# Order of the last block's routing and the second expert tile's split, and which engine splits two tiles' second weights

## The chip, the cores and the metric

The kernel runs on one core of one Trainium2 chip. The metric is the device time of one execution in microseconds (us); the time of the kernel before is the median of three runs. All inputs and the output lie in the chip's memory.

## The reference, cut to what matters

Three stages follow each other over 3072 tokens of width 256.

```
# 1. a state-space attention, chunk by chunk -> x, 3072 x 256
# 2. a dense layer
h = x @ w_in                      # 256 -> 2048
x = max(0.01 * h, h) @ w_out      # 2048 -> 256
# 3. a layer of 8 experts, one expert per token
logits = x @ w_gate + modality_bias[modality_id]
e_idx  = argmax(logits)
gate_w = softmax(logits)[e_idx]   # with 1e-9 in the sum
for e in range(8):                # w1: 8 x 256 x 1024, w2: 8 x 1024 x 256
    rows = (e_idx == e)
    out[rows] = gate_w[rows] * (max(x[rows] @ w1[e], 0) @ w2[e])
```

Everything is float32. Every product is made on TensorE from two halves: a high part `hi` (rounded to the type that TensorE reads) and a low part `lo = raw - hi`; three matmuls (hi x hi, hi x lo, lo x hi) make one product.

## The kernel before, in words

**Stages and blocks.** The tokens are cut into six blocks of 512. Per block and per 128 columns of the hidden layer, `mm1` (line 585) makes six matmuls into `h`, ScalarE and VectorE turn `h` into `gh` and `gl`, and `mm2` (line 605) makes six matmuls into `y`. The attention of the next block is threaded through this loop. A dictionary `sched` (line 926) says after which `mm1` each other step is written; lines 984 to 994 are the loop.

**Routing of a block.** `evict_y` copies the block's `y` out of PSUM to `yt`. `logits` (line 626) makes 16 small matmuls `lp`, copies them (`lt`), transposes them (`l`) and calls `route` (line 641): ten small VectorE instructions `lg` to the reciprocal into `ysb`, with one ScalarE exponential `ex` among them; `oh` and `ohb` hold the chosen expert. `ranks` (line 668) counts with small matmuls `rp` which place each token has in its expert's list, and four GpSimd scatters write the token's number into the list `il`. `rows` (line 702), called twice per block, transposes `yt` back to one row per token (`yr`) and ScalarE copies it to `ysb`; `rows_out` (line 713) writes `ysb` to the table of rows `yx`. `table_early` (after block 4) and `table_final` (line 766, after block 5) work out, from the counts, which expert and which list position each expert tile has.

**Expert tiles.** The expert layer is worked in tiles of 256 rows of one expert. Twelve are always done: five from the early table (tokens of the first five blocks), seven from the final one; more are done under a condition at the end. A tile has these steps: `m2_idx` (line 794) loads the tile's list entries (`gi`) and gathers its rows from `yx` (`xg`); `m2_w` (line 782) loads the weights to `r1` and `r2` through SyncE's queue; `m2_xT` (line 827) transposes the rows (`xps`) and splits them into `x2h` and `x2l`; `m2_split1` (line 812) splits the first weights into `w1s`; `m2_split2` (line 821) splits the second weights into `w2s`, in two halves; `m2_mm1` (line 840) makes 48 matmuls into `hp`, with ScalarE and VectorE making `hh` and `hl` from it; `m2_mm2` (line 859) makes 48 matmuls into `o`, and the result is scaled and scattered to the output. A split (line 525) is one ScalarE copy for the high part and one subtraction for the low part. The subtraction runs on VectorE for `w1s` and for the first half of `w2s`, on GpSimd for the second half of `w2s`, in every tile.

**Where the change sits.** After the loop over blocks the list `fin` (lines 998 to 1001) orders the steps of the last block (`jl`, block 5) and of the first two tiles. With the three positions inserted it reads: evict_y, logits, m2_xT of tile 1, ranks, table_final, rows 0, rows 1, m2_mm1 of tile 0, rows_out, m2_split1 of tile 1. The loop of lines 1005 to 1017 then writes, per tile: `m2_mm1(i)`, `m2_xT(i+1)`, `m2_split1(i+1)`, the loads for tile i+2, `m2_mm2(i)`, `m2_split2(i+1)`. Tile 0's `m2_split2` is written inside the loop over block 5 (line 980), tile 1's in the first pass of the loop over tiles.

**What sets the order.** The program is handed to a planner that orders each engine's instructions by its own estimate of when their inputs are there; the written order decides between instructions that are ready. An instruction called through `v`, `s`, `g` or `t_` (VectorE, ScalarE, GpSimd, TensorE) is tied behind the one written before it on the same engine when the step's name stands in `pin` with that letter (lines 64 to 95, `run` in line 172). In `fin` this ties VectorE's instruction of `m2_xT`, TensorE and ScalarE in `rows`, VectorE, ScalarE and GpSimd in `table_final` and `evict_y`, and ScalarE in `m2_split1`; `logits`, `ranks` and `m2_mm1` are tied by nothing. Once planned, each engine runs its queue in order. `lp`, `xps` and `yr` share one PSUM buffer (tag "m", one buffer): a later one of them waits until the one before has been read.

Of the kernel before, what the change touches and what calls it, by code (L numbers as in the profile page):

```python
# [24 lines left out]
Q = {'sg': (0, 1),  # L25
 'i00': 0,
 'i01': 1,
 'lo1': -1,
 'o00': 0,
 'o01': 4,  # L30
 'i10': 3,
 'i11': 3,
 'xe': 2,
 'se': 8,
 'me': 7,
 'sh1': -2,
 'sh': 0,
 'ld': 9,
# [60 lines left out]
def kernel(  # L99
# [70 lines left out]
    v, s, g, t_ = Pinned(nc.vector, "v"), Pinned(nc.scalar, "s"), Pinned(nc.gpsimd, "g"), Pinned(nc.tensor, "t")  # L170
# [354 lines left out]
    def split(raw, hi, lo, eng):  # L525
        s.copy(out=hi, in_=raw)
        eng.tensor_tensor(out=lo, in0=raw, in1=hi.bitcast(F32), op=ALU.subtract)
# [77 lines left out]
    def mm2(j, f):  # L605
        n = blocks[j][1]
        if f == 0:
            y_t[j] = [psy.tile([P, 512], F32, tag="y", name="y") for _ in range(2)]
        gh, gl = g_t.pop((j, f))
        for k in range(2):  # L610
            ds = slice(k * P, (k + 1) * P)
            for i, (w, gg) in enumerate(((woh, gh), (woh, gl), (wol, gh))):
                t_.matmul(y_t[j][k], lhsT=w[:, f, ds], rhs=gg, start=(f == 0 and i == 0), stop=(f == NF - 1 and i == 2))
# [207 lines left out]
    def m2_split2(i):  # L821
        d = m2[i]
        for k in range(2):
            ks = slice(4 * k, 4 * k + 4)
            split(d["r2"][:, ks, :], d["w2"][:, ks, 0, :], d["w2"][:, ks, 1, :], v if k == 0 else g)

    def m2_xT(i):
        d = m2[i]
# [148 lines left out]
    for i in range(EARLY):  # L977
        at(L + 1, m2_idx, i, tabe, i)
    at(L + 4, m2_split1, 0)
    at(L + 6, m2_split2, 0)  # L980
    at(L + 9, m2_w, 1, tabe, 1)
    at(L + Q["xt"], m2_xT, 0)
# [12 lines left out]
    jl = nb - 1  # L995
    mm2(jl, NF - 2)
    mm2(jl, NF - 1)
    fin = [(evict_y, jl), (logits, jl), (ranks, jl), (table_final,), (rows, jl, 0), (rows, jl, 1), (rows_out, jl)]
    fin.insert(Q["xe"], (m2_xT, 1))
    fin.insert(Q["se"], (m2_split1, 1))  # L1000
    fin.insert(Q["me"], (m2_mm1, 0))
    for fn, *args in fin:
        run(fn, args, "L_")
    tl = [(tabe, k) for k in range(EARLY)] + [(tabf, k) for k in range(NSTAT)]
    for i in range(len(tl)):
        if i:
            run(m2_mm1, (i,), "L_")
            if i + 1 < len(tl):
                run(m2_xT, (i + 1,), "L_")
                run(m2_split1, (i + 1,), "L_")  # L1010
        if i + 2 < len(tl):
            if i + 2 >= EARLY:
                m2_idx(i + 2, *tl[i + 2])
            m2_w(i + 2, *tl[i + 2])
        run(m2_mm2, (i,), "L_" if i + 1 < len(tl) else "Z_")
        if i + 1 < len(tl):
            run(m2_split2, (i + 1,), "L_")
    u = nc.values_load(tabu, min_val=0, max_val=NFIN, skip_runtime_bounds_check_because=WHY)

    def cond(k):  # L1020
        if k >= NFIN:
            return
        with tc.If(u > k):
            i = EARLY + k
            m2_idx(i, tabf, k)
            m2_w(i, tabf, k)
            m2_split1(i)
            m2_split2(i)
            m2_xT(i)
            m2_mm1(i)  # L1030
            m2_mm2(i)
            cond(k + 1)
# [34 lines left out]
```

## Time and profile before

| | us |
|---|---|
| median of three runs | 552.48 (550.47 to 555.38) |
| the profiled execution, its own time | 552.29 |
| its span, first to last instruction | 550.6 |
| TensorE busy in the span | 519.3 (94%) |
| VectorE busy | 365.0 (66%) |
| ScalarE busy | 334.0 (61%) |
| GpSimd busy | 199.2 (36%) |

1.7 us of the profiled execution's time lie around its span. TensorE is PE, VectorE is DVE, ScalarE is ACT, GpSimd is POOL, SyncE is SP; PEld is TensorE's weight load, which overlaps its matmuls. The expert tiles fill the last 150 us of the span; a tile's 48 matmuls `hp` are followed by its 48 matmuls `o`.

### The profile page before, as it was taken

How to read it: one execution, taken by the hardware profiler on the slowest of the kernel's cores; microseconds unless marked ns; L12 is line 12 of the kernel's file. 1: busy time of each engine (PE TensorE's matmuls, PEld its weight loads, DVE VectorE, ACT ScalarE, POOL GpSimd, SP SyncE). 2: the span in 40 equal slices, each digit the busy share in tenths (PEclk: the TensorE clock that was granted, in tenths of full speed). 3: DMA queues.
4: the chain of work that ended last, by engine and by line, in shares of the span. 5: the costliest groups of instructions: out<-in, count | busy, mean ns of one | idle time of the engine just before them, and what ended most of it. 6: DMA issues, size and time to landing. Idle time of an engine off the chain costs nothing.

```text
span 550.6 us, 9529 instructions
## 1 busy us (share of the span) xinstructions
PE 519.3 (94%) x3411; PEld 422.3 (77%) x3411; DVE 365.0 (66%) x714; ACT 334.0 (61%) x699; POOL 199.2 (36%) x167
## 2 busy tenths in 40 slices
PE   6998978999999999999999999999989999999990
PEld 3434654678787878778877787688879999999990
DVE  5658998977667777775667866475577564555630
ACT  5447667675676676765766665354537665666630
POOL 5648798300301120113010301540063466556331
PEclk9559999999999999999999999999999999999996
DMA  8898753212744239322620476345059667777300
GB/s 195 138 226 160 206 143 57 54 34 34 17 116 81 59 43 107 63 59 11 130 60 0 13 139 198 98 31 86 1 187 168 222 210 239 219 236 240 109 23 21
DMA packets 128312, 61.02 MB, mean 111 GB/s; under 512 B 84545, under 2 KB 120514, under 8 KB 128258
## 3 DMA queue, kind: packets, MB, share of 16 engines
q1 hardware_dynamic: 125186, 53.94, 48.2%
q0 software_dynamic: 3072, 6.41, 3.6%
q8 instruction: 29, 0.48, 0.4%
q14 instruction: 25, 0.20, 0.2%
HBM read 53.73 MB, written 6.60 MB: 110 GB/s over the span
## 4 chain that ended last, share of the span: by engine, by line
PE 78%; DVE 8%; issue 5%; ACT 3%; DMA 2%; SPq 1%; POOL 1%; POOLq 0%; DVEq 0%; ACTq 0%
PE y L163 21%; PE h L163 21%; PE hp L163 11%; PE o L163 10%; PE psy L163 5%; PE cb L163 3%; DVE hb L163 1%; DVE gg L163 1%; DMA ct<-in_C_dram 1%; DMA raw<-in_moe_w_in_dram 1%; DVE gl L163 1%; DVE lb L163 1%; PE yr L163 1%; PE pc L163 1%; PE pb L163 1%
## 5 line engine op out<-in xcount | busy, mean ns | idle before, releaser
L163 ACT CAST gh<-gg 128x512 fp32r<-128x512 f32 x96 | 59.6, 621 | 75.6 <-DVE gg L163 74.3
L163 DVE TENSOR_TENSOR gl<-gg,gh 128x512 fp32r<-128x512 f32 x96 | 74.0, 771 | 40.6 <-ACT gh L163 40.0
L163 PE MATMUL h<-xh,wih 128*128 128x512 f32 x192 | 77.7, 408 | 3.9 <-DVE gg L163 3.9
L163 PE MATMUL y<-gl,woh 128*128 128x512 f32 x192 | 76.6, 400 | 3.6 <-DVE gl L163 3.6
L163 DVE TENSOR_TENSOR gg<-sa,h 128x512 f32<-128x512 f32 x96 | 65.3, 681 | 20.5 <-ACT sa L163 20.2
L163 POOL TENSOR_SCALAR_AFFINE_SELECT e<-e 128x1024 f32<-128x1024 f32 (+1 forms) x28 | 28.2, 1012 | 137.9 <-DMA e<-cumd 87.1
L163 PE MATMUL h<-xl,wih 128*128 128x512 f32 x192 | 75.2, 392 | 0.0
L163 PE MATMUL y<-gh,wol 128*128 128x512 f32 x192 | 75.0, 392 | 0.0
L163 PE MATMUL h<-xh,wil 128*128 128x512 f32 x192 | 75.0, 392 | 0.0
L163 PE MATMUL hp<-x2h,w1s 128*128 128x256 f32 x384 | 71.9, 283 | 0.0
L163 PE MATMUL o<-w2s,hh 128*128 128x256 f32 x384 | 69.3, 285 | 0.0
L163 ACT ACTIVATE sa<-h 128x512 f32<-128x512 f32 x96 | 57.2, 596 | 19.0 <-PE h L163 18.4
L163 DVE SCALAR_TENSOR_TENSOR hl<-hp,hh 128x512 fp32r<-128x512 f32 x48 | 33.0, 691 | 52.6 <-ACT hh L163 44.0
L163 PE MATMUL y<-gh,woh 128*128 128x512 f32 x192 | 63.3, 398 | 0.0
L163 PEld LDWEIGHTS hp<-x2h,w1s 128*128 128x128 f32 x384 | 61.1, 192 | 0.6
L163 POOL TENSOR_TENSOR w2s<-r,w2s 128x1024 fp32r<-128x1024 f32 x12 | 34.0, 2838 | 72.7 <-ACT w2s L163 48.7
L163 PEld LDWEIGHTS o<-w2s,hh 128*128 128x128 f32 x384 | 58.4, 191 | 0.4 <-issue 0.4
L163 PE MATMUL hp<-x2l,w1s 128*128 128x256 f32 x192 | 53.3, 283 | 0.0
L163 ACT ACTIVATE hh<-hp 128x512 fp32r<-128x512 f32 x48 | 28.4, 597 | 40.0 <-PE hp L163 35.0
L163 ACT ACTIVATE e<-e,ncum 128x128 f32<-128x128 f32 x160 | 51.5, 395 | 0.0
L163 PE MATMUL o<-w2s,hl 128*128 128x256 f32 x192 | 51.1, 283 | 0.0
L163 POOL DMA_INDIRECT il<-ids,pi x24 | 25.7, 1070 | 66.5 <-DVE pi L163 38.3
(205 smaller groups left out, 1012.3 us busy)
## 6 DMA issues: line engine op xcount, KB each, us to landing
r<-in_moe_w_dram SPq DMA_DIRECT2D x48, 512.0 KB
e<-cumd SPq DMA_DIRECT2D x20, 512.0 KB
raw<-in_moe_w_in_dram SPq DMA_DIRECT2D x4, 1024.0 KB
raw<-in_moe_w_out_dram SPq DMA_DIRECT2D x4, 1024.0 KB
yx<-ysb SPq DMA_DIRECT2D x6, 528.0 KB
xt<-in_x_dram SPq DMA_DIRECT2D x24, 128.0 KB
ct<-in_C_dram SPq DMA_DIRECT2D x24, 64.0 KB
bt<-in_B_dram SPq DMA_DIRECT2D x24, 64.0 KB
```

Source lines behind the costliest of these rows:

```text
L163: r = f(*args, **kw)
```

## The change

`m2_xT` of tile 1 is written before the last block's `logits`; `ranks` and `table_final` are written at the end of `fin`, behind both `rows`, `m2_mm1` of tile 0, `rows_out` and `m2_split1` of tile 1. The three positions go out of `Q`. For tiles 0 and 1 the second half of `w2s` is subtracted on VectorE instead of GpSimd; the other tiles keep GpSimd.

```
-            split(d["r2"][:, ks, :], d["w2"][:, ks, 0, :], d["w2"][:, ks, 1, :], v if k == 0 else g)
+            split(d["r2"][:, ks, :], d["w2"][:, ks, 0, :], d["w2"][:, ks, 1, :], v if k == 0 or i < 2 else g)
...
-    fin = [(evict_y, jl), (logits, jl), (ranks, jl), (table_final,), (rows, jl, 0), (rows, jl, 1), (rows_out, jl)]
-    fin.insert(Q["xe"], (m2_xT, 1))
-    fin.insert(Q["se"], (m2_split1, 1))
-    fin.insert(Q["me"], (m2_mm1, 0))
+    fin = [
+        (evict_y, jl), (m2_xT, 1), (logits, jl), (rows, jl, 0), (rows, jl, 1), (m2_mm1, 0), (rows_out, jl), (m2_split1, 1),
+        (ranks, jl), (table_final,),
+    ]
```

## Rows read from the trace of the kernel before

**Rows 1.** Stretches: length, busy time (instructions) PE, PEld, DVE, ACT, POOL; clock, DMA share, GB/s.

```profile
365.00:380.00 15.00, 15.00 (x74) 12.44 (x73) 10.29 (x12) 8.05 (x13) 3.45 (x2) 1.00 0.92 108
394.00:412.00 18.00, 15.38 (x141) 14.41 (x140) 14.35 (x42) 8.93 (x14) 9.46 (x7) 1.00 0.42 133
436.00:520.00 84.00, 84.00 (x706) 84.00 (x705) 48.42 (x57) 53.56 (x79) 47.16 (x34) 1.00 0.67 212
```

**Rows 2.** Who waited for whom on PE from 300 us on: total, times, longest.

```profile
PE rp L163 <- DVE ohb L163: 2.1, 1, 2.1
PE h L163 <- DVE gg L163: 1.2, 1, 1.2
PE yr L163 <- DVE x2l L163: 0.5, 1, 0.5
```

**Rows 3.** Timeline of PE, 394 to 418: start, length, instruction, count, idle before and releaser.

```profile
394.19 0.41 PE L163 MATMUL lp<-yt,wg 128*32 128x128 f32 x2
...
401.70 0.63 PE L163 MATMUL hp<-x2h,w1s 128*128 128x256 f32 x4
404.44 0.19 PE L163 MATMUL rp<-ohb,tris 128*128 128x32 bf16 x1 [2.11 <-DVE ohb L163]
...
405.31 0.66 PE L163 MATMUL yr<-ident,yt 128*128 128x128 f32 x4 [0.52 <-DVE x2l L163]
...
411.51 0.40 PE L163 MATMUL o<-w2s,hh 128*128 128x256 f32 x2
...
417.69 0.28 PE L163 MATMUL hp<-x2h,w1s 128*128 128x256 f32 x1
```

**Rows 4.** Timeline of DVE around the stall.

```profile
393.47 0.69 DVE L163 COPY yt<-y 128x512 f32<-128x512 f32 x1 [0.41 <-PE y L163]
...
397.09 2.35 DVE L163 TENSOR_TENSOR w1s<-r,w1s 128x1024 fp32r<-128x1024 f32 x2
399.36 3.41 DVE L163 TENSOR_TENSOR w2s<-r,w2s 128x1024 fp32r<-128x1024 f32 x1
402.69 0.18 DVE L163 TENSOR_TENSOR lg<-l,btab 128x32 f32<-128x32 f32 x1
...
404.20 0.18 DVE L163 CAST ohb<-oh 128x32 bf16<-128x32 f32 x1
...
404.60 0.66 DVE L163 TENSOR_TENSOR x2l<-xps,x2h 128x512 fp32r<-128x512 f32 x1
```

**Rows 5.** VectorE's instructions that write w2s: min/median/max ns, first and last start.

```profile
L163 DVE TENSOR_TENSOR w2s<-r,w2s x12: 1205/1220/3409, 366.8 to 523.6; 128x1024 fp32r<-128x1024 f32 x12
```

**Rows 6.** Timelines of POOL and DVE: the second halves of tiles 1 and 0.

```profile
398.88 2.81 POOL L163 TENSOR_TENSOR w2s<-r,w2s 128x1024 fp32r<-128x1024 f32 x1 [28.60 <-ACT w2s L163]
...
367.79 2.48 POOL L163 TENSOR_TENSOR w2s<-r,w2s 128x1024 fp32r<-128x1024 f32 x1 [1.82 <-ACT w2s L163]
...
368.25 2.57 DVE L163 TENSOR_TENSOR gl<-gg,gh 128x512 fp32r<-128x512 f32 x1 [0.24 <-ACT gh L163]
```

**Rows 7.** Chain that ended last, tile 2's first pass: start, us, what.

```profile
417.86 5.76 PE hp L163 x48
```

**Rows 8.** Timeline of DVE, the table's first and last instruction and tile 2's first split.

```profile
405.34 0.19 DVE L163 TENSOR_SCALAR cm<-thr 1x96 f32<-1x96 f32 x1
...
414.24 0.67 DVE L163 SCALAR_TENSOR_TENSOR hl<-hp,hh 128x512 fp32r<-128x512 f32 x1
414.84 0.15 DVE L163 CAST tabf<-vb 1x14 int32<-1x14 f32 x1
414.91 0.67 DVE L163 TENSOR_TENSOR x2l<-xps,x2h 128x512 fp32r<-128x512 f32 x1
415.51 2.34 DVE L163 TENSOR_TENSOR w1s<-r,w1s 128x1024 fp32r<-128x1024 f32 x2
```

**Rows 9.** Timelines of SP and POOL: tile 5's list entries, the last list scatter.

```profile
429.93 0.37 SPq L797 DMA_DIRECT2D gi<-il  x1
...
410.33 0.97 POOL L163 DMA_INDIRECT il<-ids,pi  x1 [0.30 <-issue]
```

More of the change, by code (lines that the diff above doesn't have):

```diff
@@ L32 @@
  'i11': 3,
- 'xe': 2,
- 'se': 8,
- 'me': 7,
  'sh1': -2,
```

## The prediction

> **What bounds the kernel now.** I read the stretches first: how much of each TensorE was busy, and at which granted clock. In the expert tiles, from 436 to 520, TensorE is busy for 84.00 of 84.00 us at clock 1.00; in block 5's loop, 365 to 380, for 15.00 of 15.00 [rows 1]. Where it is never idle, only fewer or faster matmuls would shorten the run, and the change touches no matmul's size or number. The one stretch with room is 394 to 412, the handover from block 5 to the tiles: 15.38 busy of 18.00, so 2.62 us idle. TensorE's waits say what that was: 2.1 us of `rp` for `ohb`, 0.5 us of `yr` for `x2l`, and, from 300 on, otherwise only 1.2 us in front of an `h` that the change does not touch [rows 2]. So 2.1 + 0.5 = 2.6 us is the most that removing these waits can give.
>
> TensorE's timeline shows how it came about. At 401.70 tile 1 begins with four `hp`, which need only `x2h`; the next thing in the queue is block 5's `rp`, which waits 2.11 us to 404.44; then `yr`, which waits another 0.52 us because `x2l` still reads the shared buffer; only then does `hp` go on [rows 3]. From 401.70 to tile 1's first `o` at 411.51 it takes 9.81 us, where tile 2's 48 `hp` take 5.76 [rows 3, 7].
>
> VectorE's timeline shows what they waited for. It subtracts `w1s` from 397.09 and `w2s` from 399.36, and this one half of `w2s` takes 3.41 us; then comes the chain `lg` (402.69) to `ohb` (404.20), and last `x2l` at 404.60 [rows 4]. The other halves take 1.22 us at the median [rows 5]. So tile 1, whose weights had been split, stood behind block 5's routing twice: `rp` ahead of its `hp` in TensorE's queue, and its `x2l` tied behind the routing in VectorE's.
>
> **The change, part by part.**
>
> *The rows of tile 1 ahead of the logits.* `x2l` is tied behind VectorE's instruction written before it. That was the last of the routing, which is why it starts right after it at 404.60; it becomes the copy `yt`, which ends at 393.47 + 0.69 = 394.16 [rows 4]. With 0.66 us of its own it is done at about 394.8, 7 us ahead of the 401.70 at which `hp` asks for it. The 0.5 us wait of `yr` goes, and `hp` of tile 1 can run without the routing. The price is the shared buffer: the transposes of tile 1 now hold it before `lp`, which ran at 394.19 [rows 3]. `lp` may so come 394.8 - 394.19 = 0.6 us later. Its cost to TensorE lies between 0 (the planner puts `o` of tile 0, ready then, in front) and 0.6; a gain is excluded, since nothing asked for `lp` earlier. I take 0.2, nearer to the row that has `o` ready to fill in. If this cover is gone it is the whole 0.6.
>
> *The second half of `w2s` of tiles 1 and 0 on VectorE.* Tile 1's GpSimd half ran from 398.88 to 401.69; VectorE's half, which started inside it at 399.36, ended at 402.77, 1.08 us after GpSimd's end, about the 1.22 us of an undisturbed one [rows 4 to 6]. In tile 0 the same: GpSimd from 367.79 to 370.27, and the `gl` that started at 368.25 took 2.57 us to 370.82, where an instruction of its shape takes 0.67 [rows 6, 8]. So VectorE lost 3.41 - 1.22 = 2.19 us and 2.57 - 0.67 = 1.90 us. Moving the half costs it 1.22 each time: net 0.97 and 0.68 us less. In tile 0 it is worth nothing, since TensorE is busy throughout that stretch [rows 1]; if the extra half fell badly, it would cost at most its 1.22 us. In tile 1 it lets the chain `lg` to `ohb` end about 1.0 us earlier, even if all four halves stand before it.
>
> The Trainium skill, "SBUF — State Buffer", section "SBUF: two separate sides", says that VectorE instructions with two SBUF inputs and GpSimd instructions that read SBUF lock each other out for a whole instruction. By that rule the stretches above end with the move. Were the 3.41 us the instruction's own, VectorE would instead spend 1.22 us more, and the gain below would shrink from 2.6 to about 1.4 us.
>
> *Ranks and final table last.* This moves on VectorE five small instructions of `ranks` and the table's 22, which ran between 405.34 and 414.84 among the `hl` of tile 1 [rows 8]; on TensorE eight small `rp`; on GpSimd four list scatters, of which the last ran at 410.33; on SyncE nothing, though `rows_out` no longer stands behind them. `rp` need no longer stand ahead of tile 1's `hp`, whose inputs are all there, and so the 2.1 us wait goes. Whether the planner puts it a little too early is open: between 0 and the 2.1 us of before; I take 0.1, because the instruction that ran late is the one just shortened. Nothing asks early for what is moved: the list entries of tile 5, the first that need the full list and the final table, are loaded at 429.93 [rows 9], 15 us behind the table's end and 18.6 us behind the last scatter's. That slack hides a delay of the POOL queue and of the table; past it SyncE would hold tile 5's weights up too.
>
> *The two `rows` earlier* brings two sets of four transposes and two ScalarE copies forward, the same work, and the row table to memory sooner. Nothing.
>
> **The sum.** The profiled execution took 552.29 us, 0.2 under the median of 552.48; its span is 550.6. Out of it come 2.6 us of waits; back come 0.2 (`lp`) and 0.1 (`rp`): 2.3 us. Every later tile runs without a gap, so this reaches the end whole: 552.29 - 2.3 = 550.0 us, a gain of 0.4%.
>
> **The rivals.**
>
> *VectorE becomes the bound (the gain is halved).* It is busy 14.35 of 18.00 us in this stretch [rows 1]. Tile 2's `x2l` is tied behind the last `hl` of tile 1, and `w1s` of tile 2 follows, to 417.85, just as TensorE begins tile 2 at 417.69 [rows 3, 8]: no slack. If VectorE's order stays as it was and only the 1.0 us worked out above is saved, tile 2 begins 1.0 us earlier, not 2.6: 551.3 us. For it: the tightness. Against it: the table is no longer wanted first, and `hl` come earlier. The Trainium skill, "Perfetto Trace Analysis", section "Optimizing Scalar/DVE Operations", says that a saturated VectorE may be relieved by giving work to ScalarE or even GpSimd; the moved halves go the other way, and no run here shows it.
>
> *The wait only changes its name (no change).* The written order is only a preference: the planner may again put `rp`, or the second `yr` that waits for ScalarE's copy behind the routing, ahead of `hp`. The change then does not do what it says, and TensorE idles about as long: 552.3 us. Against it: `x2l` is tied elsewhere, which no estimate can undo.
>
> *Slower: the table ahead of tile 2's weights.* `rp` goes behind all of tile 1's `hp`, which would end at about 411.5 - 2.6 = 408.9; `rp` and `ranks` end at about 410.2 (0.4 + 5 x 0.18). The table's 22 instructions, written ahead of tile 2's steps, then take some 5 us (22 of 0.15 are 3.3; the 9.65 us from first to last less four `hl` are 7.0), two late `hl` 1.3, `x2l` 0.6 and `w1s` 2.34: 419.4, where it ended at 417.85. It decides from the point at which tile 2's `w1s` ends behind 417.85; here it is 1.6 us: 553.9 us. Against it: `ohb` is ready long before, and `rp` is short.
>
> *More than the waits.* A newly planned order also closes the 1.2 us in front of `h`, or loosens block 5's loop: 548.8 us or less. The stretch that would have to give it is full.
>
> **Chances.** Forecast 0.56, halved 0.20, no change 0.11, slower 0.08, more 0.05. The forecast's own range is 549.4 to 550.5 (all of the 2.6 plus rounding, and `lp` and `rp` at 0.6 and 1.0). The runs of before spread from 550.47 to 555.38, so a median moves by a microsecond or so by itself. From 547.6 the range takes in half of "more", and to 553.2 the halved and the unchanged case with that movement; outside are the slower case and the far ends. About 1%, 5.5 us, is what a measurement of this kernel can tell from no change. No case worked out reaches it on either side: 0.05 for faster, left for a re-planned block 5, and 0.05 for slower, for a mishap in the planned order; within it 0.90.
>
> **What would show it.** Right: in the changed profile 394 to 410 shows TensorE idle for under 0.5 us; no `rp` or `yr` among its waits over 0.3 us; `x2l` of tile 1 near 394; no half of `w2s` of tiles 0 and 1 over 1.3 us and no `gl` of 2.5 us; tile 2's `hp` starting near 415. Wrong: a wait of `hp` for `w1s` of tile 2 (VectorE the bound), a wait of `yr` for `ysb` or of `lp` for `x2l` over 0.6 us (the shared buffer), a wait of `rp` for `ohb` as before, or idle time inside block 5's loop, where none was.

## The result and the profile after

The changed kernel takes 559.5 us (558.78 to 561.05, four runs) beside 553.51 for the kernel before in the same comparison: 1.011 times, interval 1.0079 to 1.0141. It is slower, where 550.0 was forecast, in a range of 547.6 to 553.2. The profiled execution took 559.1 us, its span is 557.4. A time given below is the median of all runs of a kernel, while a ratio, with its interval in brackets, is taken against runs of the kernel before made beside it and leaves out the few runs in a slower state (one in experiment 7, two in experiment 8, one of the kernel before).

Who waited for whom on TensorE from 300 us on, in the changed kernel; the three waits of before [rows 2] are all gone, and two others stand in their place:

```profile
PE o L160 <- ACT hh L160: 6.1, 1, 6.1
PE o L160 <- DVE hl L160: 1.3, 1, 1.3
```

The timeline of TensorE in the changed kernel, tile 2 (compare [rows 3]; columns as there):

```profile
416.14 0.36 PE L160 MATMUL hp<-x2h,w1s 128*128 128x256 f32 x1
...
423.93 0.39 PE L160 MATMUL o<-w2s,hl 128*128 128x256 f32 x1 [1.32 <-DVE hl L160]
...
430.81 0.80 PE L160 MATMUL o<-w2s,hh 128*128 128x256 f32 x2 [6.14 <-ACT hh L160]
431.40 0.41 PE L160 MATMUL o<-w2s,hl 128*128 128x256 f32 x1
431.62 0.63 PE L160 MATMUL o<-w2s,hh 128*128 128x256 f32 x2
```

Tile 2 begins well, and then its second pass stands still for 6.14 us. Behind the gap two `o` take 0.42 us from start to start of the next (431.62, then 432.04), where 0.24 is usual. The stretches show why (columns as [rows 1]; the clock is the third number from the end):

```profile
394.00:412.00 18.00, 17.91 (x160) 17.02 (x160) 14.57 (x40) 10.14 (x17) 3.62 (x4) 1.00 0.47 161
...
420.00:422.00 2.00, 2.00 (x19) 2.00 (x19) 1.93 (x7) 0.50 (x2) 1.55 (x3) 1.00 0.88 74
422.00:424.00 2.00, 0.68 (x7) 0.48 (x5) 1.87 (x4) 0.00 (x0) 2.00 (x1) 1.00 1.25 87
424.00:426.00 2.00, 0.67 (x4) 0.47 (x4) 0.00 (x0) 0.00 (x0) 0.13 (x1) 0.77 0.46 68
426.00:428.00 2.00, 0.00 (x0) 0.00 (x0) 0.00 (x0) 0.00 (x0) 0.00 (x0) 0.50 0.74 194
428.00:430.00 2.00, 0.00 (x0) 0.00 (x0) 0.00 (x0) 0.79 (x1) 0.00 (x0) 0.50 1.01 380
...
434.00:436.00 2.00, 2.00 (x14) 2.00 (x13) 0.11 (x1) 0.00 (x0) 0.17 (x1) 0.67 0.80 229
436.00:438.00 2.00, 2.00 (x19) 2.00 (x18) 0.00 (x0) 0.20 (x1) 0.44 (x1) 1.00 0.97 374
```

The handover, 394 to 412, is full now: 17.91 of 18.00, against 15.38 before [rows 1]. But TensorE stands still for 1.32 us from 422.6 and for 6.14 us from 424.7; its granted clock falls from 1.00 (2.4 GHz) to 0.50 (1.2 GHz), and it stays there to about 435, after work has begun again. From 430.81 to 435.03 the trace holds 19 matmuls, 0.22 us each instead of 0.12: 1.9 us lost. Between 426 and 428 no compute engine is busy at all. Only the DMA engines are, and between 420 and 426 they move 68 to 87 GB/s, after it 194 and 380.

ScalarE's timeline in the changed kernel says what everything waits for:

```profile
416.80 0.84 ACT L160 ACTIVATE o<-o,xg 128x256 f32<-128x256 f32 x2
417.52 0.59 ACT L160 CAST x2h<-xps 128x512 fp32r<-128x512 f32 x1
417.99 2.02 ACT L160 CAST w1s<-r 128x1024 fp32r<-128x1024 f32 x2
419.89 0.61 ACT L160 ACTIVATE hh<-hp 128x512 fp32r<-128x512 f32 x1
429.21 1.05 ACT L160 CAST w2s<-r 128x1024 fp32r<-128x1024 f32 x1 [8.71 <-DMA r<-in_moe_w_dram]
430.16 0.59 ACT L160 ACTIVATE hh<-hp 128x512 fp32r<-128x512 f32 x1
430.65 1.04 ACT L160 CAST w2s<-r 128x1024 fp32r<-128x1024 f32 x1
431.59 1.09 ACT L160 ACTIVATE hh<-hp 128x512 fp32r<-128x512 f32 x2
```

The `hh` are tile 2's; the `x2h` at 417.52 and the `w1s` and `w2s` behind it are tile 3's. The planner put tile 3's first copy of `w2s` in front of three of tile 2's four `hh`. That copy waited 8.71 us for its weights to land, and TensorE waited for the `hh` behind it. In the kernel before, the same stretch reads:

```profile
420.77 0.60 ACT L163 ACTIVATE hh<-hp 128x512 fp32r<-128x512 f32 x1 [1.69 <-PE hp L163]
...
423.66 0.60 ACT L163 ACTIVATE hh<-hp 128x512 fp32r<-128x512 f32 x1 [0.60 <-PE hp L163]
424.28 0.59 ACT L163 CAST x2h<-xps 128x512 fp32r<-128x512 f32 x1
424.76 2.00 ACT L163 CAST w1s<-r 128x1024 fp32r<-128x1024 f32 x2
426.66 2.00 ACT L163 CAST w2s<-r 128x1024 fp32r<-128x1024 f32 x2
```

Four `hh` first, then tile 3's copies, and the weights are there when they are wanted.

The 1.32 us in front of the first `hl` come from the same fault in VectorE's queue. In the changed kernel it subtracts tile 3's `w1s` ahead of tile 2's `hl`:

```profile
420.86 1.20 DVE L160 TENSOR_TENSOR w1s<-r,w1s 128x1024 fp32r<-128x1024 f32 x1
422.07 1.21 DVE L160 TENSOR_TENSOR w1s<-r,w1s 128x1024 fp32r<-128x1024 f32 x1
423.20 0.67 DVE L160 SCALAR_TENSOR_TENSOR hl<-hp,hh 128x512 fp32r<-128x512 f32 x1
```

**Where the 6.8 us of span went.** The two profiled executions differ already at the end of the first block (VectorE's first `yt` at 118.6 against 116.0), long before any changed instruction; at the last `yt` it is 395.78 against 393.47, 2.3 us. About 1.0 of these is work that only stands earlier: four transposes of tile 1 and five `hp` of tile 0 now run ahead of that `yt` (from it to the last `o` the trace has 1186 matmuls before and 1177 after); against it the 1.2 us wait of `h` is gone [rows 2]. From that `yt` to tile 2's first `hp` it is 20.36 us after the change and 24.22 before: 3.9 us gained, of which 2.5 are idle time that is gone, 0.6 those five `hp`, and 0.7 that the other matmuls follow each other faster (0.3 of it the 16 `lp`, which stand in one piece now). From there to the last `o` (544.67; 536.64 before) 128.5 against 119.0: 9.6 us lost, which are 1.3 + 6.1 of waits, 1.9 of half speed and 0.3 unexplained. The end behind the last `o` is 1.2 us shorter. So 2.3 - 3.9 + 9.6 - 1.2 = 6.8. Because the starts differ from run to run, the profiles below are compared from the last `yt` to the last `o`: 143.2 us before, 148.9 after.

The load that came late was asked for earlier than in the kernel before, 416.73 against 417.88. SyncE's and GpSimd's timelines in the changed kernel:

```profile
416.73 0.95 SPq L786 DMA_DIRECT2D r<-in_moe_w_dram  x2
420.33 4.38 SPq L783 DMA_DIRECT2D r<-in_moe_w_dram  x2
...
414.38 1.77 POOL L160 DMA_INDIRECT il<-ids,pi  x1 [0.30 <-issue]
```

The last list scatter ran at 414.38 to 416.15, 4 us later than before [rows 9], just ahead of that load. Two theories follow, of which each may hold alone or with the other. **Q, the queue:** the loss is the order of ScalarE's queue, where copies for tile 3 stand ahead of tile 2's `hh`. **S, the scatters:** the load is late because bulk transfers crawl after list scatters. Their rival **D** is the one of the prediction: VectorE, with two more halves and a later table.

### The profile page after: what moved, and what is told of

Read it like the earlier page. It is cut to its first block, busy times and chain, and to the rows that moved or that the text cites. A ratio compares the mean times of both kernels' runs of the same rounds, so it can differ in the third digit from the quotient of the medians.

```text
span 557.4 us, 9520 instructions
## 1 busy us (share of the span) xinstructions
PE 519.9 (93%) x3411; PEld 424.4 (76%) x3411; DVE 363.6 (65%) x716; ACT 333.5 (60%) x699; POOL 195.6 (35%) x165
## 4 chain that ended last, share of the span: by engine, by line
PE 78%; DVE 7%; DMA 5%; issue 4%; ACT 2%; POOL 1%; SPq 0%; POOLq 0%; DVEq 0%; ACTq 0%
PE y L160 21%; PE h L160 21%; PE o L160 11%; PE hp L160 10%; PE psy L160 5%; PE cb L160 3%; DMA r<-in_moe_w_dram 2%; DVE gl L160 2%; DMA e<-cumd 1%; DMA raw<-in_moe_w_in_dram 1%; DVE gg L160 1%; PE pc L160 1%; PE yr L160 1%; DVE hb L160 1%; DVE lb L160 1%
## 5 line engine op out<-in xcount | busy, mean ns | idle before, releaser
L160 DVE TENSOR_TENSOR gl<-gg,gh 128x512 fp32r<-128x512 f32 x96 | 70.9, 739 | 40.4 <-ACT gh L160 39.1
L160 PE MATMUL o<-w2s,hh 128*128 128x256 f32 x384 | 71.2, 290 | 6.2 <-ACT hh L160 6.1
L160 PEld LDWEIGHTS o<-w2s,hh 128*128 128x128 f32 x384 | 60.0, 196 | 6.8 <-ACT hh L160 6.3
L160 PEld LDWEIGHTS h<-xh,wih 128*128 128x128 f32 x192 | 36.5, 191 | 14.2 <-DVE gg L160 5.8
```

The lines of the kernel that those rows point to most:

```text
L160: r = f(*args, **kw)
```

## The experiments

**1. ScalarE's copy of the rows tied as well.** All the change, with one letter more: it ties `x2h` behind the four `hh` written before it.

```
-         'L_m2_xT': 'v',
+         'L_m2_xT': 'vs',
```

> The changed kernel with ScalarE's copy x2h of m2_xT tied, too, behind the instruction written before it: ScalarE's queue then holds all four hh of tile 2 ahead of x2h, w1s and w2s of tile 3; all else of the change stays (table last, four halves on VectorE). Theory Q (the loss is a queue: the copy of tile 3's second weights, whose load is late, stands ahead of three hh that TensorE wants): the waits of o for hh and hl (6.1 and 1.3 us) and the half-speed matmuls behind them (20 at 0.215 instead of 0.12 us, 2 us) go, so about 559.5 - 9.4 = 550 us, a ratio to before of 0.993 to 0.997. Rival D (VectorE's added halves and the table on it late, the loss forecast as a rival): a wait of hp or o for VectorE's w1s, w2s or hl of over 3 us stays and the time is 556 us or more.

550.32 us, 0.9957 of before (0.9924 to 0.9989). The long wait is gone, though not every one: `o` still waits 1.6 us for `hh`. ScalarE's timeline in this kernel:

```profile
420.90 0.60 ACT L160 ACTIVATE hh<-hp 128x512 fp32r<-128x512 f32 x1 [0.24 <-PE hp L160]
421.40 0.58 ACT L160 CAST x2h<-xps 128x512 fp32r<-128x512 f32 x1
421.86 2.01 ACT L160 CAST w1s<-r 128x1024 fp32r<-128x1024 f32 x2
428.88 1.05 ACT L160 CAST w2s<-r 128x1024 fp32r<-128x1024 f32 x1 [5.01 <-DMA r<-in_moe_w_dram]
```

The load, asked for at 415.82, is as late as in the changed kernel (13.1 us to the copy). Now it stands behind tile 2's `hh` and delays tile 3's only. VectorE's subtractions need ScalarE's copies, and so its queue changed with the tie; tile 2's four `hl` now come first:

```profile
420.06 2.47 DVE L160 SCALAR_TENSOR_TENSOR hl<-hp,hh 128x512 fp32r<-128x512 f32 x4
...
423.05 2.34 DVE L160 TENSOR_TENSOR w1s<-r,w1s 128x1024 fp32r<-128x1024 f32 x2
```

So Q holds for the two queues together, and this run does not tell them apart. D's 556 us and its wait of over 3 us did not come; experiments 3, 4 and 9 decide about its added halves and its late table.

**2. No list scatters for the last block.**

```
-        for q in range(nq):
+        for q in range(nq if j < len(blocks) - 1 else 0):
             w = g.indirect_dma_start(out=il[:], ...
```

> The changed kernel without the last block's four list scatters, so that block's tokens are missing from the lists and their output rows are not written; ScalarE's queue keeps the order of the changed kernel. Theory S (the load of tile 3's second weights is late because bulk transfers crawl, at 60 to 140 GB/s for some 8 us, after list scatters): with no scatters that load, asked for at about 416.7, runs at over 300 GB/s and lands by about 421 to 422; o waits for hh at most 1 us instead of 6.1, and the time is about 551 us. Rival (the load is late for another reason: its own small packets, or too many loads at once): it still lands near 429 and the time stays within 1 us of the changed kernel's.

The last block's tokens are then missing from the lists; the order of copies, subtractions, `hh` and `hl` on ScalarE and VectorE is that of the changed kernel.

554.48 us. The load asked for at 415.48 has landed by 419.75, 4.3 us later, with 323 GB/s in 418 to 420 where the changed kernel has 143, and 74 in the 2 us after that. No `o` waits for `hh`. So S holds for the load. The time fell by 5.0 us where S expected some 8, since VectorE's queue has the same fault. The copy on ScalarE, and the subtraction on VectorE that costs TensorE most:

```profile
419.75 1.05 ACT L160 CAST w2s<-r 128x1024 fp32r<-128x1024 f32 x1 [0.50 <-DMA r<-in_moe_w_dram]
...
422.57 3.83 DVE L160 TENSOR_TENSOR w2s<-r,w2s 128x1024 fp32r<-128x1024 f32 x1
```

The subtraction is tile 3's first half, ahead of three `hl` of tile 2, and beside GpSimd's half (422.90, 2.40 us) it takes 3.83 us instead of 1.22. `o` waits 3.9 us for `hl` in this run: 1.3 behind `w1s`, as in the changed kernel, and 2.6 behind this half. After it the clock reads 0.71 over 426 to 428 and 0.50 over 428 to 430, so a stretch at half clock comes without the late load too.

**3. The written order alone**, second halves on GpSimd as before (`v if k == 0 else g`).

> Only the new written order; the second halves of w2s stay on GpSimd in all tiles. ScalarE's planned queue has all four hh of tile 2 ahead of tile 3's copies here. Theory Q: no wait of o for hh, so the gain of the order alone is seen: rp no longer ahead of hp, but VectorE's half of tile 1 still stretched to some 3.4 us beside GpSimd's; about 550 to 552 us. Rival D with the table as the cause: the loss stays, 556 us or more, since the table is as late here.

549.44 us, 0.9935 (0.9899 to 0.9971): faster than before. The handover is full (18.00 of 18.00), and no wait of TensorE is over 0.4 us. The table is late here too, so the late table is not the loss. One step of the expectation missed: VectorE's half of tile 1 took 1.22 us (396.57), and GpSimd's, which started behind it (396.98), took 3.04. Which of the two is stretched was not worked out: in experiment 2 VectorE's started 0.33 us ahead and was the one stretched.

**4. The halves alone**, in the written order of before.

> Only the two second halves on VectorE; the written order is that of the kernel before. Theory Q: ScalarE's queue is unharmed, so no loss; VectorE's half of tile 1 takes 1.22 instead of 3.41 us, the chain to ohb ends about 1 us earlier and the 2.1 us wait of rp shrinks to 0.5 to 1.5 us: about 552 to 553 us. Rival D with the halves as the cause: a new wait on VectorE of 3 us or more, 556 us or more.

551.64 us, 0.999 (0.9955 to 1.0025): no difference that the runs show. The halves are not the loss either. The wait of `rp` for `ohb`, expected at 0.5 to 1.5 us, is gone from this profile; 0.7 us of `hp` for `x2h` and 0.4 of `yr` for `x2l` are there.

**5. Two of the four scatters.** As in 2, with 2 in place of 0.

> The changed kernel with two of the last block's four list scatters left out (half of that block's tokens are missing from the lists). Theory S with a price per scattered entry: bulk transfers crawl for about 4 us instead of 8 behind the scatters, the load of tile 3's second weights lands some 8 us after its issue (12.5 with four scatters, 4.3 with none), o waits for hh 1 to 3 us and the time lies between 554.5 (none) and 559.5 (four), at 556 to 558 us. Rival (the crawl comes with any scatter, whatever their number): landing 12 us after the issue, 559 us.

554.54 us. From issue to the copy it is 8.8 us (414.29 to 423.12), so 4.3, 8.8 and 12.5 us for none, two and four scatters of 128 entries: about 2.1 us each. `o` waits 2.5 us for `hh` and 1.3 for `hl`, together 3.8, as much as with no scatters; the order of the queues alone costs that, and so the time is not clearly higher than in 2 (1.0061, 1.0031 to 1.0092, beside 1.0035, 1.0003 to 1.0067), where 556 to 558 was expected.

**6. One move alone:** tile 1's rows ahead of the logits, all else as before.

```
-    fin.insert(Q["xe"], (m2_xT, 1))
+    fin.insert(1, (m2_xT, 1))
```

> The kernel before with one step moved: m2_xT of tile 1 ahead of logits; ranks and table where they were, second halves on GpSimd. ScalarE's planned queue has tile 3's x2h, w1s and w2s ahead of three hh of tile 2, as in the changed kernel. Theory Q: this one move is enough for the loss; o waits for hh 2 to 6 us (the scatters come earlier than in the changed kernel, so the load may land sooner), 554 to 559 us. Rival (the loss needs the late table and ranks or the halves on VectorE): 550 to 552 us, as with the order alone.

561.04 us, 1.0183 (1.012 to 1.0245), at least as slow as the whole change (1.0079 to 1.0141). ScalarE's timeline in this kernel has the fault again, with the copy of `w2s` ahead of the `hh`:

```profile
419.09 0.60 ACT L163 ACTIVATE hh<-hp 128x512 fp32r<-128x512 f32 x1
428.81 1.04 ACT L163 CAST w2s<-r 128x1024 fp32r<-128x1024 f32 x1 [9.12 <-DMA r<-in_moe_w_dram]
429.76 0.59 ACT L163 ACTIVATE hh<-hp 128x512 fp32r<-128x512 f32 x1
```

`o` waits 7.2 us for `hh`. Neither the late table nor the halves are needed for the loss. Here the scatters ended at 410.8, and the row table, asked for at 409.18, crawled in front of the weights (13 to 38 GB/s from 412 to 418). This run has a second loss, which the changed kernel has not (a row of its waits, and one of its stretches):

```profile
PE xps L163 <- issue: 2.0, 1, 2.0
...
416.00:418.00 2.00, 2.00 (x12) 2.00 (x11) 1.37 (x2) 2.00 (x4) 1.23 (x1) 0.50 1.03 38
```

Tile 3's transposes start at 413.68, 1.95 us behind the matmul before them and just when tile 2's `x2l`, which reads the shared buffer, ends (413.62); behind this wait TensorE works at half clock (416 to 418). So the 153.6 us of this profile are not the price of the ScalarE order alone.

**7. List entries of 64 bytes** in the changed kernel: 16 equal numbers instead of one.

```
-    il = dram.tile([NE * NT, 1], I32, name="il")
+    il = dram.tile([NE * NT, 16], I32, name="il")
...
-                in_=ids[:, c0 + q:c0 + q + 1], in_offset=None,
+                in_=ids[:, c0 + q, :], in_offset=None,
```

The first fill of the list grows with it, from 96 to 1536 KB, and a tile's load of its entries takes the first number of each.

> The changed kernel with list entries of 64 bytes instead of 4: a scatter writes 128 whole entries of 16 numbers, the loads of a tile's entries take the first number of each, and the fill of the list is 16 times as large (1.5 MB, early in the run). ScalarE's queue is that of the changed kernel. Theory P (the crawl is the price of 4-byte writes): it goes, the load of tile 3's second weights lands 4 to 5 us after its issue, and the time is near the one without scatters, 554 to 556 us (plus up to 2 us if the larger fill delays the start). Rival (the price goes by the number of scattered entries): still 12 us to landing, 559 us or more.

552.74 us, 1.0015 (0.9976 to 1.0054). With all four scatters in place the load lands 4.1 us after its issue (415.11 to 419.20), as with none:

```profile
419.20 1.05 ACT L160 CAST w2s<-r 128x1024 fp32r<-128x1024 f32 x1 [0.33 <-DMA r<-in_moe_w_dram]
```

So the crawl is the price of the 4-byte writes. What is left is 3.9 us of `o` waiting for `hl`, as in 2: 1.3 behind `w1s` and 2.5 behind the same half in VectorE's queue (422.19, 3.83 us).

**8. The order alone, with 64-byte entries.**

> Only the new written order (second halves on GpSimd in all tiles, as in the run of the order alone) and list entries of 64 bytes. Theories Q and P together: no wait of o for hh, and ScalarE no longer stands 3.5 us in front of tile 3's second weights; TensorE's idle of 0.7 us in 424 to 436 goes: 548.5 to 549.5 us, a ratio to before of about 0.992. Rival: the larger fill or the strided loads of the entries cost more than they give, 550 us or more.

546.2 us, 0.9897 (0.9858 to 0.9935).

**9. The whole change with both remedies.**

> The changed kernel with both remedies: x2h tied, and list entries of 64 bytes. If queue and late load are the whole loss, no wait of o for hh or hl over 0.5 us is left, TensorE is never idle from 394 to the last o, the stretch from the last block's yt to the last o falls to about 140 us (143.2 before, 148.9 after), and the time is 546 to 548 us, as with the order alone and wide entries. Rival (VectorE's halves cost something of their own): 549 us or more.

546.26 us, 0.9901 (0.9863 to 0.9938). Both beat the kernel before and the changed one. In this kernel TensorE has no wait at all from 300 us on, though the late table and the added halves on VectorE are still there, and so D falls. The stretches read:

```profile
394.00:412.00 18.00, 18.00 (x160) 17.99 (x159) 14.35 (x44) 9.69 (x17) 8.88 (x7) 1.00 0.52 168
412.00:424.00 12.00, 12.00 (x103) 12.00 (x102) 8.85 (x14) 8.04 (x12) 7.34 (x5) 1.00 0.79 265
424.00:436.00 12.00, 12.00 (x103) 12.00 (x102) 7.31 (x9) 7.67 (x13) 7.22 (x6) 1.00 0.75 224
```

**10. The kernel before with 64-byte entries.**

> The kernel before with list entries of 64 bytes and nothing else. If the slow transfers behind the scatters cost the kernel before nothing (its loads landed in time), the time stays within 2 us of before, and the order alone is what the best version gains; if they cost something that the profile of before does not show, 548 to 550 us.

550.47 us, 0.9971 (0.9942 to 1.0001): within 2 us, as expected if the crawl cost the kernel before nothing. Its waits of 2.1 and 0.5 us are unchanged. With 64-byte entries the planner orders VectorE otherwise from 5.5 us on, so part of the gain of 8 and 9 may lie at the start of the run; this is not shown.

From the last `yt` to the last `o`, one profile each:

| kernel | us | ratio of times to before |
|---|---|---|
| before | 143.2 | 1 |
| changed | 148.9 | 1.011 |
| 1 change, `x2h` tied | 142.8 | 0.9957 |
| 2 change, no scatters | 144.7 | 1.0035 |
| 3 order alone | 140.9 | 0.9935 |
| 4 halves alone | 141.1 | 0.999 |
| 5 change, two scatters | 145.8 | 1.0061 |
| 6 tile 1's rows first alone | 153.6 | 1.0183 |
| 7 change, 64-byte entries | 144.8 | 1.0015 |
| 8 order, 64-byte entries | 139.8 | 0.9897 |
| 9 change, tied, 64-byte entries | 139.0 | 0.9901 |
| 10 before, 64-byte entries | 143.2 | 0.9971 |

The profiles of 8 and 9 also fell on executions that began quickly; that part is no effect shown here, and the column leaves it out. In the changed kernel and in 1, 2, 5, 7 and 9 nine matmuls, about 1.0 us, stand ahead of the last `yt` that stand behind it in the kernel before (in 4 six, about 0.7); beside that kernel these rows look that much better than they are.

Four of the rows make a square of the two remedies on the changed kernel: 148.9 with neither, 142.8 with the tie, 144.8 with wide entries, 139.0 with both. The tie takes off 6.1 or 5.8 us and the wide entries 4.1 or 3.8, so the two together take off 9.9 us, all that the changed kernel lost behind its handover.

## Why the prediction was wrong

**What held.** The bound was read rightly, and the handover did what was forecast. VectorE's timeline in the changed kernel:

```profile
395.78 0.69 DVE L160 COPY yt<-y 128x512 f32<-128x512 f32 x1 [0.79 <-PE y L160]
396.38 0.68 DVE L160 TENSOR_TENSOR x2l<-xps,x2h 128x512 fp32r<-128x512 f32 x1
...
400.65 2.35 DVE L160 TENSOR_TENSOR w2s<-r,w2s 128x1024 fp32r<-128x1024 f32 x2
...
418.24 2.09 DVE L160 TENSOR_TENSOR kt<-kt,dt 1x14 f32<-1x14 f32 x1
```

`x2l` of tile 1 follows `yt` at once. The two halves take 2.35 us together, none is stretched. `lp` came 3.7 us behind `yt`, where it had come 0.7 behind it and 0.6 more was forecast, but it made TensorE wait for nothing (0.2 was taken), and so did `rp` (0.1). The rule of the Trainium skill ("SBUF — State Buffer", section "SBUF: two separate sides") was the right one to take: the last row above, an instruction with two inputs over 14 numbers, takes 2.09 us instead of 0.15 and ends at 420.33, while GpSimd's half of tile 2 runs (416.98 to 420.30).

**The term that was too small.** With both remedies the stretch is 4.2 us shorter (143.2 to 139.0), of which about 1.0 is the work moved ahead of it, so 3.2 us reach the end; with the order alone and wide entries, where the stretch holds as many matmuls as before (1186), it is 3.4. Forecast were 2.3: the 2.6 of the waits less 0.3. The 0.3 were not needed, and the rest is that matmuls follow each other faster, 0.7 us up to tile 2, which the sum did not have. One sum of the prediction is wrong beside this: `lp` and `rp` at 0.6 and 1.0 give 551.3 as the upper end of its own range, not 550.5; the outcome does not hang on it.

**The step that failed** is one sentence of the sum: "Every later tile runs without a gap, so this reaches the end whole." It took the planned order of ScalarE's queue in tiles 2 and 3 for given, as the profile of before showed it. But only some instructions are tied. Tile 3's `x2h` and `w2s` were not, and their place ahead of tile 2's `hh` depends on when the planner believes that their inputs are there. Moving one step, experiment 6, moved them two tiles later. Experiments 1 and 6 show this from both sides. In place of a gain of 2.3 us that reaches the end, tile 2 lost 7.4 us of waits and 1.9 of half speed.

**The second failed step** is "That slack hides a delay of the POOL queue and of the table". It priced the scatters only by who reads the list. What they do to the transfers behind them was not in the sum, and it turned waits of 3.9 us (experiments 2 and 7) into 7.4, and cost 4.1 us of the stretch (148.9 beside 144.8). The profile of before held the sign. After the scatters its DMA engines were as busy as in the tiles (the last number but one; 0.67 from 436 to 520 [rows 1]), and moved 17 to 56 GB/s from 414 to 420:

```profile
414.00:416.00 2.00, 2.00 (x19) 2.00 (x18) 1.97 (x7) 2.00 (x3) 0.00 (x0) 1.00 0.72 17
...
418.00:420.00 2.00, 2.00 (x19) 2.00 (x19) 0.98 (x1) 0.57 (x2) 2.00 (x1) 1.00 1.08 56
```

There it met the row table, for which nobody waited.

**The rivals.** The slower rival had the right sign and the wrong place: tile 2's `w1s` on VectorE, which ended at 416.7 and so ahead of the point of decision, 417.85. The case of no change had said that the written order is only a preference, and the chances held 0.05 for "a mishap in the planned order", but neither was walked through: none looked at ScalarE's queue behind the handover, none past tile 2's start. The signs listed as proof of an error did not include the one that came, a wait of `o` for `hh`.

## What to carry to other kernels

Where a planner orders the engines' queues, a moved step may reorder work that it does not touch: look in each engine's queue for an instruction that waits for a transfer and stands ahead of one that the busiest engine needs, and tie the waiting one behind it. Price a transfer that is moved not only by who waits for its data but by what it does to the transfers behind it. A gain at a handover counts only when the next two handovers have been walked through at their new times.

## What the runs showed of the hardware

A scatter of 128 entries of 4 bytes held up the load behind it for about 2.1 us (4.3, 8.8 and 12.5 us to landing with none, two and four); with entries of 64 bytes the hold-up was gone (4.1 with four). The price is that of the changed kernel and does not fit experiment 6, where behind four scatters first the row table crawled and then the weights took 12.5 us as well. The Trainium skill ("DMA: Bandwidth & Descriptors", section "Specifications") says that below 512 bytes a transfer becomes a read-modify-write. No run here shows whether that is the cause: the trace has a scatter of 4-byte entries as 16 packets of 32 bytes and one of 64-byte entries as 16 packets of 512, so by its packets experiment 7 is at that bound and by its entries under it. Why 4-byte writes hold up the others is not shown.

TensorE's clock fell while it waited 6.14 us in the changed kernel (0.77 over 424 to 426, 0.50 over 426 to 428) and read 1.00 again from 436 on, when work had gone on since 430.81. The length of the wait alone does not say whether it falls. The 2.11 us wait of the kernel before left it at 1.00 [rows 1]; behind the 1.95 us wait of experiment 6 and a 1.61 us wait of experiment 1 it read 0.50 (416 to 418; 437 to 439) while TensorE was busy throughout. In experiment 1 the 15 matmuls that started from 436.34 to 439.32 took 0.21 us each instead of 0.12, so the 1.61 us of the wait cost some 1.4 us more behind it.
